# A second copy engine for the first x block, and a 416 + 96 split of the last output piece, in a GEGLU feed-forward kernel

## The chip, the cores and the metric

The kernel runs on one core of one Trainium2 chip. The metric is the device time of one execution in microseconds (us). In the profile, PE is TensorE's matmul work, PEld its weight loads, DVE VectorE, ACT ScalarE and POOL GpSimd; ACTq and SPq are the queues of ScalarE and SyncE that issue DMAs. To evict is to copy a finished sum out of PSUM; the pitch is the time from one matmul's start to the next one's. The profile covers the span from the core's first to its last instruction; it is about 1.8 us shorter than the device time (299.16 and 297.4 us in the profiled run before).

## The reference

```
B, S, D, F = 32, 32, 1024, 3584                     # bf16
def reference(x, w_gate, w_up, w_down):
    return (gelu(x @ w_gate) * (x @ w_up)) @ w_down # gelu with the tanh approximation
```

So 1024 rows of x go through two products of 1024 by 3584 and one of 3584 by 1024.

## The kernel before

The operations are recorded in a list per engine. A helper derives the semaphore waits from the keys that each operation reads (`r`) and writes (`w`). The same key can stand for a PSUM bank: a matmul that writes bank b waits for the engine that last read bank b.

TensorE needs x transposed, with the 1024 input columns in eight blocks of 128 on the partitions. Blocks 2 to 7 come through a transposing DMA. Blocks 0 and 1 are wanted sooner: 512 rows of them are loaded plainly into `xn`, transposed by TensorE into PSUM and copied out. The gate and up matmuls of block 0 come next. The kernel's PSUM tile `ps`, which every matmul writes, has eight banks, and bank 2m (gate) and 2m+1 (up) hold the sums of weight column m = 0..3.

```python
for n in [512] * 6 + [128] * 2:          # warm-up matmuls on constants, bank 3
    pr.add("pe", "matmul", ps[:, 3, 0:n], one[:, 0:P], one[:, 0:n], start=True, stop=True, w=[("ps", 3)])
for i, eng in enumerate(("sp", "act")):  # half of x's first 512 rows on each DMA queue
    pr.add(eng, "dma_start", xn[:, 2*i:2*i+2, :], x_r[:, 2*i:2*i+2, 0:NX*P], w=[("xn", i)], dma=f"xn{i}")
# ... weight and x loads are cut ...
pr.add("act", "activation", warm[:, 0:1], const0, ACTF.Gelu_apprx_tanh)   # brings the table load here
for k in range(NX):                      # NX = 2 blocks
    for i, b in enumerate((6, 7) if k == 0 else (4, 5)):
        half = ps[:, b, 0:P].bitcast(BF16)
        for t in range(2):
            pr.add("pe", "transpose", half[:, t*P:(t+1)*P], xn[:, 2*i+t, k*P:(k+1)*P], ident[:, :],
                   r=[("xn", i), "ident"], w=[("ps", b)])
        pr.add("dve", "tensor_copy", xT[:, k, i*256:(i+1)*256], half, r=[("ps", b)],
               w=[("x", k, 0) if i == 0 else ("x", k, "b")])
# ... the gate, up and most of the down matmuls are cut ...
jobs += [[(TC-1, 0, 512)], [(TC-1, 512, 256)], [(TC-1, 768, 256)]]   # last 128 rows: three pieces
# each piece: 28 matmuls, then a copy from PSUM (ScalarE and VectorE in turn), then its output DMA
```

## Time and profile before

| | before |
|---|---|
| median of 6 runs | 299.86 us (299.33 to 300.19) |
| span of the profiled run | 297.4 us |
| first gate matmul starts | 4.61 us |
| last matmul starts | 294.65 us |
| from there to the end | 2.73 us |

The page of the kernel before gives the busy time of each engine and the shares of the chain of waits that ended last:

```profile
PE 292.7 (98%) x1362; PEld 79.3 (27%) x808; DVE 42.5 (14%) x68; ACT 37.5 (13%) x67; POOL 0.7 (0%) x6
...
PE 98%; issue 0%; ACT 0%
```

In the timeline each line has a start and a duration in us, the engine, the operation and, in brackets, the idle time before it with what ended that idle time. These are the lines of the head of the kernel before, gathered from narrow windows of its timeline (weight loads, matmuls, the first two VectorE copies, ScalarE):

```profile
0.74 0.47 ACTq L98 DMA_DIRECT2D xn<-in_x_dram  x1
...
3.52 1.28 ACT L98 ACT_TABLE_LOAD   x1 [3.52 <-issue]
4.82 0.20 ACT L98 ACTIVATE warm<-const-float32-0.0 128x1 f32<-128x1 f32 x1
...
3.96 0.29 DVE L98 COPY xT<-ps 128x256 bf16<-128x256 bf16 x1 [3.96 <-PE ps L98]
...
4.17 0.29 DVE L98 COPY xT<-ps 128x256 bf16<-128x256 bf16 x1
...
4.58 0.56 PEld L98 LDWEIGHTS ps<-xT,wg 128*128 128x128 bf16 x4 [0.29 <-issue]
...
4.61 0.38 PE L98 MATMUL ps<-xT,wg 128*128 128x512 bf16 x1
```

The second copy ends at 4.47 and the first gate matmul follows at 4.61. Four weight loads follow one another without a wait between them, and a matmul of 512 columns is drawn 0.38 us long. Starts of such matmuls are 215.7 ns apart, which is the measure of their cost; the drawn length overlaps the next one.

The tail of the kernel before, again from its timeline:

```profile
294.65 0.27 PE L98 MATMUL ps<-wd,hT 128*128 128x256 bf16 x1
294.96 0.38 ACT L98 ACTIVATE xT<-ps 128x256 bf16<-128x256 f32 x1 [5.52 <-PE ps L98]
295.37 0.33 SPq L98 DMA_DIRECT2D out_dram<-xT  x1
```

From its groups by shape, the matmuls of the two last pieces (count, then busy us, mean ns, idle us before); then, from its DMA view, the last issue (KB, us to landing):

```profile
L98 PE MATMUL ps<-wd,hT 128*128 128x256 bf16 x56 | 6.3, 272 | 0.0
...
out_dram<-xT SPq DMA_DIRECT2D x1, 64.0 KB, 1.6
```

The last matmul starts at 294.65; ScalarE evicts the piece, the DMA is issued and lands 1.61 us later, and the span ends 0.40 us after that.

### The profile page before, as it was taken

The page shows a single profiled execution, that of the slowest core. Times are in us where ns is not written, and L with a number is a line of the kernel's source. Part 1 is how long each engine was busy: PE and PEld are TensorE (multiplying, and loading weights), DVE is VectorE, ACT ScalarE, POOL GpSimd, SP SyncE. Part 2 cuts the span into 40 slices and gives each one's busy share as a digit, 9 for nine tenths or more (in the row PEclk, how much of TensorE's full clock was granted, in tenths as well). Part 3 has the DMA queues.
Part 4 walks back from the last instruction along what each step waited for, and adds up shares of the span by engine and source line. Part 5 has one row for each costly group of instructions (what it writes and reads, how often), then busy time and mean ns, then how long its engine had stood idle before and what let it go on. Part 6 is the DMA issues. An engine that isn't in the chain of part 4 may idle for free.

```text
span 297.4 us, 2549 instructions
## 1 busy us (share of the span) xinstructions
PE 292.7 (98%) x1362; PEld 79.3 (27%) x808; DVE 42.5 (14%) x68; ACT 37.5 (13%) x67; POOL 0.7 (0%) x6
## 2 busy tenths in 40 slices
PE   8999999999999999999999999999999999999996
PEld 4444222222222222222222222222222222222255
DVE  1030311112211111111111221110000000000000
ACT  1030411111111111211111111110000000000010
POOL 0000000000000000000000000000000000000000
PEclk9999999999999999999999999999999999999999
DMA  7999734006608309121030030000101101001011
GB/s 201 268 247 354 237 106 142 1 0 225 198 2 304 121 10 355 62 102 39 0 141 2 0 141 0 0 2 0 35 0 37 35 0 35 15 23 35 0 35 35
DMA packets 28842, 26.37 MB, mean 89 GB/s; under 512 B 8224, under 2 KB 25248, under 8 KB 28832
## 3 DMA queue, kind: packets, MB, share of 16 engines
q1 hardware_dynamic: 26640, 24.25, 25.5%
q10 hardware_dynamic: 2192, 1.97, 2.3%
q8 instruction: 8, 0.13, 0.2%
q14 instruction: 2, 0.02, 0.0%
HBM read 22.28 MB, written 2.10 MB: 82 GB/s over the span
## 4 chain that ended last, share of the span: by engine, by line
PE 98%; issue 0%; ACT 0%
PE ps L98 56%; PE ps L163 43%; ACT xT L98 0%
## 5 line engine op out<-in xcount | busy, mean ns | idle before, releaser
L98 PE MATMUL ps<-xT,wg 128*128 128x512 bf16 x250 | 88.4, 379 | 0.3
L98 PE MATMUL ps<-xT,wu 128*128 128x512 bf16 x250 | 87.9, 379 | 0.2
L98 PE MATMUL ps<-wd,hT 128*128 128x512 bf16 (+1 forms) x272 | 83.6, 357 | 0.0
L163 PE MATMUL ps<-wd,hT 128*128 128x512 bf16 x196 | 74.3, 379 | 0.4
L163 PE MATMUL ps<-xT,wu 128*128 128x512 bf16 x189 | 71.6, 379 | 0.3
L163 PE MATMUL ps<-xT,wg 128*128 128x512 bf16 x189 | 71.6, 379 | 0.2
L98 DVE TENSOR_TENSOR hT<-g,ps 128x512 bf16<-128x512 f32 x56 | 36.3, 685 | 158.1 <-PE ps L98 152.5
L98 ACT ACTIVATE g<-ps 128x512 f32<-128x512 f32 x56 | 30.8, 595 | 159.8 <-PE ps L98 159.8
L98 PEld LDWEIGHTS ps<-wd,hT 128*128 128x128 bf16 x280 | 27.4, 98 | 69.8 <-issue 65.8
L98 PEld LDWEIGHTS ps<-xT,wu 128*128 128x128 bf16 x256 | 25.0, 98 | 71.7 <-issue 64.1
L98 PEld LDWEIGHTS ps<-xT,wg 128*128 128x128 bf16 x256 | 25.0, 98 | 71.5 <-issue 64.0
L98 DVE CAST xT<-ps 128x512 bf16<-128x512 f32 (+1 forms) x8 | 5.3, 658 | 87.7 <-ACT xT L98 79.8
L98 ACT ACTIVATE xT<-ps 128x512 bf16<-128x512 f32 (+1 forms) x9 | 5.2, 573 | 94.6 <-PE ps L98 94.6
L98 PE MATMUL ps<-const-bfloat16-1.0 128*128 128x512 bf16 (+1 forms) x8 | 2.9, 545 | 0.8 <-PEq L309 0.8
L98 ACT ACT_TABLE_LOAD x1 | 1.3, 1283 | 3.5 <-issue 3.5
L98 PEld LDWEIGHTS ps<-const-bfloat16-1.0 128*128 128x128 bf16 x8 | 1.0, 137 | 2.4 <-issue 2.4
L98 DVE COPY xT<-ps 128x256 bf16<-128x256 bf16 x4 | 0.9, 292 | 4.0 <-PE ps L98 4.0
L98 PE MATMUL ps<-ident,xn 128*128 128x128 bf16 x8 | 1.1, 311 | 0.0
L98 PEld LDWEIGHTS ps<-ident,xn 128*128 128x128 bf16 x8 | 0.8, 136 | 0.0
L98 POOL TENSOR_SCALAR_AFFINE_SELECT ident<-ident 128x128 bf16<-128x128 bf16 x1 | 0.3, 295 | 0.2 <-POOL ident L98 0.2
L98 POOL MEMSET ident<- 128x128 bf16 x1 | 0.2, 205 | 0.3 <-POOLq L309 0.3
L98 ACT ACTIVATE warm<-const-float32-0.0 128x1 f32<-128x1 f32 x1 | 0.2, 203 | 0.0
(4 smaller groups left out, 0.4 us busy)
## 6 DMA issues: line engine op xcount, KB each, us to landing
wd<-in_w_down_dram SPq DMA_DIRECT2D x7, 1024.0 KB, 5.1
wg<-in_w_gate_dram SPq DMA_DIRECT2D x6, 1024.0 KB, 7.8
wu<-in_w_up_dram SPq DMA_DIRECT2D x6, 1024.0 KB, 10.1
out_dram<-xT SPq DMA_DIRECT2D x15, 128.0 KB, 1.7
wg<-in_w_gate_dram ACTq DMA_DIRECT2D x3, 256.0 KB, 4.9
wu<-in_w_up_dram ACTq DMA_DIRECT2D x3, 256.0 KB, 5.2
wu<-in_w_up_dram ACTq DMA_DIRECT2D x2, 128.0 KB, 3.8
wg<-in_w_gate_dram SPq DMA_DIRECT2D x2, 128.0 KB, 3.3
```

The lines of the kernel that those rows point to most:

```text
L98: ins = name(eng, *args, **kw) if callable(name) else getattr(eng, name)(*args, **kw)
L163: return eng.add_instruction(mybir.InstMatmult(start_tensor_calc=start, stop_tensor_calc=stop, ldweights=False, name=nc.get_next_instructi ...
```

## The change

There are two intents. In the head, the second half of block 0 is copied out by two engines at once, so that the first gate matmul can start sooner; for this ScalarE's table load is moved to the very front. In the tail, the last piece shrinks to 96 columns, so that less is left to evict and to store when TensorE is done.

```diff
+        pr.add("act", "activation", warm[:, 0:1], const0, ACTF.Gelu_apprx_tanh)   # now ahead of the DMA issues
 ...
-        pr.add("act", "activation", warm[:, 0:1], const0, ACTF.Gelu_apprx_tanh)
         for k in range(NX):
-            for i, b in enumerate((6, 7) if k == 0 else (4, 5)):
-                (two transposes of 128 columns into bank b, one VectorE copy of 256)
+            plan = ([((0, 1), 6, "dve"), ((2,), 7, "dve"), ((3,), 5, "act")] if k == 0 else
+                    [((0, 1), 4, "dve"), ((2, 3), 2, "dve")])
+            (per entry: its transposes into its bank, then one copy by the engine named)
 ...
-        jobs += [[(TC - 1, 0, 512)], [(TC - 1, 512, 256)], [(TC - 1, 768, 256)]]
+        jobs += [[(TC - 1, 0, 512)], [(TC - 1, 512, 416)], [(TC - 1, 928, 96)]]
```

The two lines in parentheses shorten code. One further key, `("x", k, "c")`, makes the first half of the matmuls wait for ScalarE's copy as well.

## The prediction

> What bounds it now. TensorE: the page gives PE 98% busy, and the chain of waits is 98% PE. In the timeline the first gate matmul starts at 4.61 us and the last matmul at 294.65; 1344 matmuls of 512 columns (or their equal) at the traced 215.7 ns are 289.9 us of that. The middle has no slack; only the head (4.6 us) and the tail (about 2.6 us) can change.
>
> Head, before. The timeline has the transposes at a 107 ns pitch from 3.51; the four 256-column copies on VectorE start at 3.96, 4.17, 4.39, 4.60 (292 ns each), each as soon as its second transpose is done. PE's last transpose starts at 4.25; PE then waits for the second copy (ends 4.47) and goes on at 4.61. The first gate weights had landed at 4.01. At most about 0.25 us can be won.
>
> Head, after. ScalarE's copy of 128 columns, estimated from traced ACTIVATEs (597 ns at 512, 384 at 256), takes about 0.28 us; its transpose is seen done at 4.17, so it ends at 4.45, against 4.47. That gains 0.02 us, and an extra wait in PE's queue (76 ns) may eat it. Two costs are added:
> - The second copy of block 1 moves from bank 5 to bank 2, which the second gate matmul writes. The copy ends near 4.89; the matmul wants to start at about 4.81. I expect a stall of 0.1 to 0.15 us.
> - The table load (1283 ns) and warm-up activation now stand before ScalarE's DMA issues. The second half of x landed at 3.62 with no slack. If the queue runs ahead of the engine, the issues move by some 0.05 us. The Trainium skill (Perfetto Trace Analysis, Per-instruction lifecycle, DVE / Act Engine Instruction) says the sequencer fetches on once an instruction is in the wait queue; the trace agrees so far as the warm-up activation starts 11 ns after the table load ends, but no DMA issue follows a running activation there. If it blocked (20%), x and the up weights would come 1.4 us later.
>
> Tail. The last pieces go from 256 + 256 to 416 + 96 columns. The traced pitch (109 ns at 256, 215.7 at 512) is columns/2.4 plus 2.4 ns; 416 + 96 cost the same sum if 96 columns reach 42 ns with a weight load each. The Trainium skill (TensorE: Matmul & The Clock Gate, Back-to-back issue gap) gives 81 ns as sustained at 128 columns; this trace shows no warm pitch below 256. At 50 ns the loss is 0.2 us, at 81 it is 1.1. The last eviction shrinks from 384 ns to about 250 (estimate, same slope), gaining 0.13 us; the last DMA's 1.6 us from issue to landing is nearly all fixed.
>
> Sum: head +0.1, tail about 0. Predicted 299.9 us, range 299.2 to 301.2; chances: faster by over 2% 0.002, within 2% 0.993, slower by over 2% 0.005.
>
> What would show it, all in the timeline: ScalarE's first DMA issue (about 0.8, or 2.2 if it blocks); the ends of the x copies; the first gate matmul (4.55 to 4.7) and its gap to the second (215 ns if bank 2 costs nothing, about 300 if it does); the pitch of the 96-column matmuls; the last ACTIVATE (about 250 ns) and the time from its end to the span's end (2.0 us, unchanged).
>
> What would make it wrong: a blocking table load; a 96-column pitch set by the weight load; slow 192-byte writes; a different moment at which TensorE's clock rises in the head; run-to-run spread (0.56 us here).

## The result and the profile after

The median is 299.88 us (299.11 to 300.54, 6 runs) against 299.86. The ratio is 1.000, with a 95% interval of 0.998 to 1.002. The spans are 297.5 and 297.4 us. The predicted time (299.9) was met. But equal times do not say that nothing happened: both ends changed, and the profile shows more than one surprise.

The engine shares after:

```profile
PE 293.1 (99%) x1362; PEld 77.8 (26%) x808; DVE 42.7 (14%) x68; ACT 37.6 (13%) x68; POOL 0.7 (0%) x6
```

The head after, the same windows of the timeline:

```profile
0.74 1.28 ACT L98 ACT_TABLE_LOAD   x1 [0.74 <-PEq L317]
0.80 0.46 ACTq L98 DMA_DIRECT2D xn<-in_x_dram  x1
...
2.03 0.20 ACT L98 ACTIVATE warm<-const-float32-0.0 128x1 f32<-128x1 f32 x1
...
4.19 0.28 ACT L98 ACTIVATE xT<-ps 128x128 bf16<-128x128 bf16 x1 [1.95 <-PE ps L98]
...
3.96 0.29 DVE L98 COPY xT<-ps 128x256 bf16<-128x256 bf16 x1 [3.96 <-PE ps L98]
...
4.17 0.21 DVE L98 COPY xT<-ps 128x128 bf16<-128x128 bf16 x1
...
4.61 0.29 DVE L98 COPY xT<-ps 128x256 bf16<-128x256 bf16 x1
...
4.58 0.10 PEld L98 LDWEIGHTS ps<-xT,wg 128*128 128x128 bf16 x1 [0.27 <-issue]
4.96 0.18 PEld L98 LDWEIGHTS ps<-xT,wg 128*128 128x128 bf16 x2 [0.28 <-DVE xT L98]
...
4.61 0.59 PE L98 MATMUL ps<-xT,wg 128*128 128x512 bf16 x1
...
4.99 0.62 PE L98 MATMUL ps<-xT,wg 128*128 128x512 bf16 x1
```

Four things are to be read here. The DMA is issued at 0.80, 0.06 us later than before, while the table load runs from 0.74 to 2.02: the load does not hold the queue back. The copy on ScalarE ends at 4.46, where the old second copy ended at 4.47. The second gate matmul starts 380 ns after the first, not 215, and the weight load before it is said to wait for VectorE, whose last copy ends at 4.90 and empties bank 2. But the matmuls are also drawn 0.59 and 0.62 us long instead of 0.38: the trace's clock record begins, at full clock, at 5.47 us in this run, against 4.59 in the run before. (It has no row for the time before; the profile's view by stretches prints 1.00 there. That TensorE runs at half clock until then is read from its pitch: 427 ns for 512 columns among the warm-up matmuls, 215.7 later.) So two explanations for the 380 ns stand side by side.

The tail after, from its timeline:

```profile
295.12 0.21 PE L98 MATMUL ps<-wd,hT 128*128 128x96 bf16 x1
295.36 0.25 ACT L98 ACTIVATE xT<-ps 128x96 bf16<-128x96 f32 x1 [5.52 <-PE ps L98]
295.64 0.33 SPq L98 DMA_DIRECT2D out_dram<-xT  x1
```

From its groups by shape, the matmuls of the last piece; from its DMA view, the last issue:

```profile
L98 PE MATMUL ps<-wd,hT 128*128 128x96 bf16 x28 | 1.4, 206 | 0.0
...
out_dram<-xT SPq DMA_DIRECT2D x1, 24.0 KB, 1.4
```

The last matmul starts at 295.12 and 2.35 us remain, against 2.73. Of the 0.38 us, 0.07 are only the shorter last matmul, whose columns moved to the piece before: at columns/2.4 plus 2.4 ns, all matmuls together cost the same, but the last one starts 0.067 us later. The real gain is 0.31 us: 0.133 from the eviction (384 to 251 ns), 0.177 from the DMA, which took 1.63 us from issue to the end of the wait for it, and now 1.45.

The sum explains the spans in ns: first gate matmul 5 earlier; 476 more from it to the last matmul (410 in the head, 66 from the later start of the last one); 377 less from there to the end. That is +94, and the spans differ by 297,473 - 297,379 = 94. The head seems to give back all that the tail gains. The question for the experiments is whether that 0.41 us is the change's doing.

### The profile page after: what moved, and what is told of

Its sections match the earlier page's. It is cut to its first block, busy times and chain, and to the rows that moved or that the text cites. A ratio compares the mean times of both kernels' runs of the same rounds, so it can differ in the third digit from the quotient of the medians.

```text
span 297.5 us, 2550 instructions
## 1 busy us (share of the span) xinstructions
PE 293.1 (99%) x1362; PEld 77.8 (26%) x808; DVE 42.7 (14%) x68; ACT 37.6 (13%) x68; POOL 0.7 (0%) x6
## 4 chain that ended last, share of the span: by engine, by line
PE 95%; SPq 2%; DMA 2%; issue 1%; ACT 0%
PE ps L98 52%; PE ps L163 43%; SPq L98 2%; DMA xT<-in_x_dram 2%; ACT xT L98 0%
## 5 line engine op out<-in xcount | busy, mean ns | idle before, releaser
L98 PE MATMUL ps<-wd,hT 128*128 128x512 bf16 (+2 forms) x272 | 83.6, 357 | 0.0
L98 PEld LDWEIGHTS ps<-wd,hT 128*128 128x128 bf16 x280 | 25.9, 98 | 71.4 <-issue 65.8
L98 ACT ACTIVATE xT<-ps 128x512 bf16<-128x512 f32 (+2 forms) x10 | 5.3, 530 | 96.5 <-PE ps L98 96.5
L98 DVE COPY xT<-ps 128x256 bf16<-128x256 bf16 (+1 forms) x4 | 0.9, 272 | 4.0 <-PE ps L98 4.0
L98 ACT ACT_TABLE_LOAD x1 | 1.3, 1283 | 0.7 <-PEq L317 0.7
```

What stands on the lines that cost most here:

```text
L98: ins = name(eng, *args, **kw) if callable(name) else getattr(eng, name)(*args, **kw)
```

## The experiments

Each kernel ran beside runs of the kernel before on the same chip; e1 to e4, e5 to e8, e9 to e12 ran on three chips. "Rise" is the moment at which the trace's clock record begins to show full clock. "Lost early" is the sum of what matmul starts in the first 3 us after the first gate matmul fall behind their full-clock pitch, whatever the cause (in e3 and e10 it is the wait for bank 2, in the others the low clock); "lost to DMA" is the same later in the head, where the waits name a load. The third column is the time from the fourth transpose (the last of block 0) to the first gate matmul; in e9, and near their end in e11, the clock rose during the transposes, which shortens it there. All are computed from the start times in the traces, in ns unless marked us.

| kernel | rise, us | 4th transpose to gate | 1st to 2nd gate | lost early | lost to DMA | last matmul to end | span, us |
|---|---|---|---|---|---|---|---|
| before | 4.59 | 786 | 215 | 0 | 0 | 2730 | 297.38 |
| after | 5.47 | 769 | 380 | 406 | 0 | 2353 | 297.47 |
| e1_bank1 | 5.64 | 769 | 379 | 498 | 193 | 2339 | 297.72 |
| e2_tail_only | 4.70 | 786 | 215 | 0 | 0 | 2351 | 297.23 |
| e3_head_only | 4.44 | 769 | 338 | 133 | 0 | 2704 | 297.57 |
| e4_after_again | 5.45 | 769 | 380 | 408 | 0 | 2338 | 297.44 |
| e5_before_again | 4.83 | 786 | 304 | 88 | 433 | 2705 | 297.87 |
| e6_tail64 | 5.36 | 790 | 382 | 351 | 0 | 2369 | 297.45 |
| e7_split_first | 5.25 | 567 | (split) | 367 | 0 | 2343 | 297.30 |
| e8_bank1_again | 4.82 | 774 | 309 | 93 | 0 | 2352 | 297.15 |
| e9_tail_again | 3.93 | 771 | 215 | 0 | 0 | 2344 | 297.04 |
| e10_after_third | no record | 769 | 341 | 136 | 1072 | 2353 | 298.26 |
| e11_split_again | 4.50 | 531 | (split) | 0 | 0 | 2342 | 297.08 |
| e12_no_warmup | no record | 788 | 378 | 1358 | 0 | 2718 | 298.98 |

### e1_bank1: the bank alone

```diff
-                    [((0, 1), 4, "dve"), ((2, 3), 2, "dve")])
+                    [((0, 1), 4, "dve"), ((2, 3), 1, "dve")])
```

> The changed kernel with one number changed: the second copy of block 1 leaves bank 1 instead of bank 2, and bank 1 is first written by the fifth matmul, not the second. Theory (the bank is a new wait): the gap from the first to the second gate matmul falls from 380 ns to the plain pitch (215 ns, or about 427 ns if TensorE's clock is still low at that moment), no wait on VectorE in front of the second matmul, and about 0.15 us less span than the changed kernel at the same clock moment. Rival (the 380 ns are the low clock alone): the gap stays at 380 or more.

The gap stayed: 379 ns, with the second weight load issued at 4.59, right behind the first matmul, and no wait. From its timeline:

```profile
4.55 0.14 PEld L98 LDWEIGHTS ps<-xT,wg 128*128 128x128 bf16 x2 [0.27 <-issue]
...
4.59 0.59 PE L98 MATMUL ps<-xT,wg 128*128 128x512 bf16 x1
```

Bank 2 was therefore not what set the 380 ns of the first profile of the change; my first reading of it falls, and the rival holds for that run. At half clock a matmul of 512 columns that starts after idle time takes some 380 ns until the next (the first warm-up matmul shows 381), and the following ones 427. Times: 299.75 us median, ratio 1.000 (0.9986 to 1.0014), which tells nothing.

### e3_head_only, e4_after_again, e8_bank1_again, e10_after_third: does bank 2 cost anything

e3 is the changed kernel with the old tail, e4 and e10 are the changed kernel once more, e8 is e1 once more.

```diff
 e3:
-        jobs += [[(TC - 1, 0, 512)], [(TC - 1, 512, 416)], [(TC - 1, 928, 96)]]
+        jobs += [[(TC - 1, 0, 512)], [(TC - 1, 512, 256)], [(TC - 1, 768, 256)]]
```

> The changed head with the old tail (256 + 256). Theory (bank 2 stall): some 0.15 us slower than before from the stall alone, 0.4 us if the late clock rise also belongs to the head's change; the first gate matmul still starts at 4.6 us. Rival (the head is neutral): within 0.1 us of before and a gap of 215 ns after the first gate matmul.

> The changed kernel once more, unchanged. If the moment at which TensorE's clock rises in the head (about 5.5 us in the first profile of it, about 4.5 in the one of before) is chance from run to run, it will differ here; if the change causes it, it is again near 5.5. The stall of about 165 ns before the second gate matmul comes back either way (in time until its weight load starts: near 4.95 us).

> Bank 1 instead of bank 2 once more, unchanged, for its head in a run in which the clock may rise early. If it rises before 4.7 us: a gap of about 215 ns after the first gate matmul, where the changed head with bank 2 had 338. If it rises late: 380 ns again, which is the low clock, and nothing is learnt of the bank.

> The changed kernel, third time. Theory (tail -0.30, copies -0.02, bank stall 0.12 where the clock has risen early and nothing where it has not, clock moment by chance): the mean of all its runs is 0.2 to 0.3 us below before, with a spread of about 1.5 us. Rival (no gain at all): pooled mean equal to that of before.

e3 caught a run in which the clock had risen early. Its weight loads and first two matmuls, from its timeline:

```profile
4.66 0.10 PEld L98 LDWEIGHTS ps<-xT,wg 128*128 128x128 bf16 x1 [0.27 <-issue]
5.03 0.11 PEld L98 LDWEIGHTS ps<-xT,wg 128*128 128x128 bf16 x2 [0.27 <-DVE xT L98]
...
4.69 0.38 PE L98 MATMUL ps<-xT,wg 128*128 128x512 bf16 x1
...
5.03 0.39 PE L98 MATMUL ps<-xT,wg 128*128 128x512 bf16 x1
```

The matmuls have their full-clock length (0.38), and the second still waits until VectorE's copy out of bank 2 has ended at 4.97. That wait costs 133 ns. e10 shows it again: 136 ns, matmuls of 0.38 us, the second weight load at 4.92 after a copy that ended at 4.87. Every old head with an early rise (before, e2, e9) has 215 ns there. In e8, with bank 1, the clock rose between the first and second matmul; here are its weight loads:

```profile
4.56 0.14 PEld L98 LDWEIGHTS ps<-xT,wg 128*128 128x128 bf16 x2 [0.27 <-issue]
4.90 0.10 PEld L98 LDWEIGHTS ps<-xT,wg 128*128 128x128 bf16 x1 [0.20 <-DVE xT L98]
```

Now the first two loads go one behind the other, so the second matmul waits for nothing; its 309 ns are the low clock of the first. (e5, an old head in which the clock rose 219 ns after the first gate matmul's start, as against 230 here, has 304. The third load is put down to VectorE because a wait on it sits there, but it starts 1 ns after the second matmul, as the loads of the kernel before do.) So bank 2 costs 0.13 us when the clock is up, and nothing when it is not (380 ns with bank 2, 379 with bank 1), because the first matmul then lasts as long as the copy. No run with bank 1 had the clock up before the first gate matmul. e8 ran once, at 298.93 us; its state is unknown, and it is one draw from a wide spread.

My expectation for e4, that a stall of 165 ns "comes back either way", was wrong as to its cause: the 380 came back, and it was the clock. e4 had a ratio of 0.998 (0.9968 to 0.9993; median 299.29), e10 one of 1.0015 (0.9999 to 1.003; 299.84), and both are the same kernel, so the interval is too narrow to judge 0.2% by. Against the before-runs, the mean of the changed kernel was 0.00, -0.62 and +0.39 us: my expectation of a pooled gain of 0.2 to 0.3 is not shown by the times (the mean of the three is -0.08). e3 had 299.47 and a ratio of 0.9999 (0.9979 to 1.002), its mean being pulled up by one run of 301.35.

### e2_tail_only and e9_tail_again: the tail alone

The kernel before, with the new line of `jobs` and nothing else.

```diff
-        jobs += [[(TC - 1, 0, 512)], [(TC - 1, 512, 256)], [(TC - 1, 768, 256)]]
+        jobs += [[(TC - 1, 0, 512)], [(TC - 1, 512, 416)], [(TC - 1, 928, 96)]]
```

> The kernel before with only the new tail (416 + 96 columns). Theory (the tail gains, the head gives it back): the part of the span from the last matmul's start to the end is 2.35 us against 2.73 before, the 96-column pitch is 42.5 ns, and the time is some 0.3 us (0.1%) below before: 299.5. Rival (the tail is neutral, as predicted): within 0.1 us of before.

> Old head with the 96-column tail, once more, beside the changed kernel and the split on one chip. Theory: 2.35 us from the last matmul's start to the end, 0.3 us below before on the sum of both places; the time 299.4 to 299.6. Rival (the gain of the first time was chance): the ratio to before is 1.000 or above.

In both traces the remainder after the last matmul's start is 2.35 and 2.34 us, and in e3, with the old tail, it is 2.70. The nine traces with 96 columns (2338 to 2353) and the four of the old tail (2704 to 2730) do not overlap. The 96-column matmuls start 42.5 ns apart. So the tail gains 0.30 us in every trace (377 less 66 in the first pair; 0.30 between the means of the groups). The times agree in one call and not in the other: 299.41 with a ratio of 0.9987 (0.9973 to 1.0001), then 299.62 and 1.0002 (0.9989 to 1.0015), which is what the rival of e9 named. The gain is shown in the traces and not in the times.

### e6_tail64: how small may the last piece be

```diff
-        jobs += [[(TC - 1, 0, 512)], [(TC - 1, 512, 416)], [(TC - 1, 928, 96)]]   # on top of e2
+        jobs += [[(TC - 1, 0, 512)], [(TC - 1, 512, 448)], [(TC - 1, 960, 64)]]
```

> The kernel before with the tail 448 + 64. Pitch theory (columns/2.4 plus 2.4 ns): 29.1 ns at 64 columns, and the sum of the last two pieces is unchanged. Rival (a floor set by the weight load): clearly more, 40 ns or above. Last ACTIVATE about 225 ns. From the last matmul's start to the end: 2.30 us if the last output DMA is free to go, or longer than the 2.35 of the 96-column tail if the 448-column piece, evicted by VectorE in about 625 ns and issued on the same queue, now holds it up.

The pitch is 29.1 ns: still columns/2.4 plus 2.4, with a weight load before each matmul and no floor. The remainder is 2369 ns, more than with 96 columns although the eviction is shorter. The two last DMA issues, from its timeline:

```profile
295.15 0.81 SPq L98 DMA_DIRECT2D out_dram<-xT  x2
```

The last eviction, from its groups by shape:

```profile
L98 ACT ACTIVATE xT<-ps 128x64 bf16<-128x64 f32 x1 | 0.2, 225 | 5.5 <-PE ps L98 5.5
```

The two issues lie one close behind the other, from 295.15 to 295.95; the second starts on time, 25 ns after the eviction, but takes 393 ns instead of 332. The packets of the 448-column piece run until 296.45, and the first packet of the last piece starts at 296.47, 0.91 us after its issue (0.83 with 96 columns). Most of that 0.08 us, 0.06, is the longer issue itself. I read this as the large piece being in the way of the small one, at the issue more than in the packets; it was not tested by moving either to another queue. Of the two sizes, 64 gains nothing over 96 in the trace. The time was 299.36, ratio 0.9977 (0.9964 to 0.999), a mean 0.65 us below before, more than this tail can give by its trace.

This run also bears on the clock. Its head is the old one, and yet the rise came at 5.36 us, with a gap of 382 ns and 351 ns lost. Its first two gate matmuls, from its timeline:

```profile
4.61 0.59 PE L98 MATMUL ps<-xT,wg 128*128 128x512 bf16 x1
...
4.99 0.56 PE L98 MATMUL ps<-xT,wg 128*128 128x512 bf16 x1
```

A late rise does not need the changed head, so the 0.41 us of the first pair cannot be put down to the change on this evidence. Whether it comes as often with both heads is open: it came after 5.2 us in three of the five changed heads that have a record, and in two of the seven others.

### e5_before_again: chance in the kernel before

> The kernel before, unchanged. Theory (the moment at which TensorE's clock rises is chance[...]): the rise can come at any moment from some 4.4 to 5.7 us, so it may be late here too, and then the first gate matmuls run at a pitch near 427 ns and the span grows by half the delay (up to 0.5 us) with nothing else changed. Rival (the changed head causes the late rise): the rise is before 4.7 us as in the first profile of this kernel.

The rise was at 4.83, between the two groups: inconclusive on that point. But the trace shows a second source of chance. From its waits between 7.5 and 13.5 us (engine, what it waited for, sum in us, times, longest):

```profile
PEld ps L98 <- DMA wg<-in_w_gate_dram: 0.8, 2, 0.5
PEld ps L98 <- DMA wu<-in_w_up_dram: 0.5, 1, 0.5
```

TensorE lost 433 ns because loads for blocks 2 and 3 landed late; the waits name the gate and up weights, and x of block 2 landed at nearly the same moment. e10 lost 1072 ns in the same way, which is why its span is 298.26. The time of e5 was 299.89, ratio 0.9992 (0.998 to 1.0004).

### e12_no_warmup: what the clock's rise hangs on

```diff
-        for n in [512] * 6 + [128] * 2:
-            pr.add("pe", "matmul", ps[:, 3, 0:n], ...)
```

> The kernel before without the eight warm-up matmuls on constants. Theory (the clock rises 3.65 to 4.9 us after TensorE starts its work, and until then each matmul takes twice as long, so the loss is half of the delay): TensorE starts at about 3.5 us, the rise comes between 7.1 and 8.4 us, and the time lost to the low clock after the first gate matmul is 1.25 to 1.9 us, so the span is 1.2 to 1.9 us longer, except where late x blocks would have made it wait anyway. Rival (the rise does not depend on TensorE's work): the rise is again between 4.4 and 5.7 us and the span is unchanged.

From the groups by shape of the window from 4.8 to 7.3 us, first this kernel, then the kernel before (last columns: busy us, mean ns):

```profile
L98 PE MATMUL ps<-xT,wg 128*128 128x512 bf16 x4 | 1.9, 622 | 0.0
L98 PE MATMUL ps<-xT,wu 128*128 128x512 bf16 x2 | 1.1, 634 | 0.0
```

```profile
L98 PE MATMUL ps<-xT,wg 128*128 128x512 bf16 x8 | 2.0, 378 | 0.0
L98 PE MATMUL ps<-xT,wu 128*128 128x512 bf16 x5 | 1.4, 379 | 0.0
```

Six matmuls fit where thirteen did before. The trace has no clock record, but the pitch turns to 216 ns near 7.6 us, 3.8 us after TensorE's first work at 3.76, and the loss is 1358 ns, half of the delay from 4.86. It was expected at 1.25 to 1.9. The time was 300.76 (one run). In the other late runs the same rule holds: after, (5.47 - 4.61)/2 = 0.43 against 0.41; e6, 0.37 against 0.35. The clock follows TensorE's work, as far as this one run without warm-up shows; with warm-up its rise came 3.2 to 4.9 us after that work began at 0.78.

### e7_split_first and e11_split_again: taking away the wait itself

The change shortens the copy. This experiment lets TensorE work during it: the old head and the 96-column tail, but the first two gate matmuls are cut into halves of 256 columns. The first halves need only the first copy. Parentheses shorten code.

```diff
+        def mm_half(m, i):
+            c0 = i * 256
+            pr.add("pe", "matmul", ps[:, 2*m, c0:c0+256], (gate weights of m, block 0), xT[:, 0, c0:c0+256],
+                   start=(i == 0), stop=False, r=[(weights), ("x", 0, "b" if i else 0)], w=[("ps", 2*m)])
 ...
+    for i in range(2):           # instead of the two matmuls m = 0, 1 of block 0
+        for j in range(2):
+            mm_half(j, i)
```

With `start` in the first half only, the result is correct.

> Old head and 96-column tail, but the first two gate matmuls are split into halves of 256 columns, first halves first, so that TensorE need not wait for the second copy of block 0. Theory (the wait for the second copy is on the critical path): the first gate matmul starts near 4.40 us instead of 4.61 to 4.78, and 0.2 us of idle time goes; the span is 0.2 us below the tail-only kernel at the same clock moment, 0.1 if the clock is still low then. Rival (it only moves the wait): a gap of the same size appears before the second halves or at the third matmul.

> The split of the first two gate matmuls with the 96-column tail, once more. Theory: from the start of the fourth transpose to the first gate matmul 0.57 us against 0.79 in every old head and 0.77 in every changed one, so the lowest span where the clock rises early (about 297.0), and a ratio to before of 0.998. Rival: the wait comes back behind the first halves.

The time from the fourth transpose to the first gate matmul falls from 786 to 567 and 531 ns, and no wait appears behind the halves: e11, with an early rise, loses nothing. From its timeline:

```profile
4.02 0.72 PE L98 MATMUL ps<-ident,xn 128*128 128x128 bf16 x6
4.63 0.60 PE L98 MATMUL ps<-xT,wg 128*128 128x256 bf16 x4
```

The four halves run as one block, 109 ns apart. (Here x itself landed late, so that the start is at 4.63 in spite of the gain. For the same reason the span of e11 is not the lowest, as I had expected: 297.08 against 297.04 in e9, whose fourth transpose started 0.28 us earlier.) The clock's moment alone changes e7 by 0.37. Times: 299.50, ratio 0.9985 (0.9971 to 1.0000), and 299.25, ratio 0.9995 (0.9978 to 1.0011). By the traces it beats both kernels: with the clock early and loads in time, the sum of head, tail and matmuls is lower than before by 0.24 (head) + 0.30 (tail) = 0.54 us, less 0.01 for the extra matmuls. The times point the same way but do not prove it: each interval reaches 1.000, and the ratio of 0.998 that I expected of e11 did not come.

## Why the prediction was right, and where not

- **What bounds it.** Right: TensorE is 99% busy after, and every difference found lies before 16 us or after the last matmul.
- **ScalarE's copy, a gain of 0.02 us.** Right: 786 to 769 ns from the fourth transpose to the first gate matmul, in all changed heads but one (774). Half of the columns hardly helps: the copy of 256 columns took VectorE 292 ns, the one of 128 takes ScalarE 277. The extra wait of 76 ns did not come: one wait instruction in TensorE's queue holds both semaphores.
- **Bank 2, a stall of 0.10 to 0.15 us.** The mechanism and the size are right where the clock is up (133 and 136 ns, absent with bank 1 and in old heads). What the prediction did not see is that a late rise hides it. The test it named, a gap of "about 300 if it does", gave 380 for another reason; a gap alone does not tell the two apart, the drawn length of the matmul does.
- **Table load, 20% risk of 1.4 us.** The likely side came: the issue moved by 0.06 us (estimate 0.05), and DMAs go out while the load runs, as the Trainium skill (Perfetto Trace Analysis, Per-instruction lifecycle) let one expect.
- **Pitch at 96 columns.** The formula read from 256 and 512 columns held (42.5 ns, and 29.1 at 64); the feared 81 ns did not come.
- **Last eviction, -0.13 us.** Right: 384 to 251 ns.
- **"The last DMA's 1.6 us from issue to landing is nearly all fixed."** This step was wrong, a mis-sized term: it fell from 1.63 to 1.45 us, and "the time from its end to the span's end (2.0 us, unchanged)" from 2.04 to 1.86. The 128 data packets took 27.2 ns each at 512 bytes and 14.9 at 192, eight to an engine, which makes 0.10 us; another 0.07 lies between the last packet and the landing (0.43 and 0.36 us); why that part shrank was not tested.
- **The sum.** "Head +0.1, tail about 0" should read head +0.12 or -0.02 (early or late clock), tail -0.30, so some 0.2 to 0.3 us of gain. The predicted 299.9 agrees with the measured 299.88, but the measurement can't tell +0.1 from -0.3: its interval is 0.6 us on either side. The forecast that the time would stay within 2% rests on solid ground; the agreement to 0.1 us is chance.
- **What the prediction listed as able to upset it**, a different moment of the clock's rise and the run-to-run spread, is larger than what was to be measured. In 14 traces the loss to a low clock was 0 to 0.50 us with warm-up, and the loss to late loads 0 to 1.07. Late loads occurred in two of the six changed heads in which the table load comes first, and in one of eight others; whether the 0.06 us later issue has a part in that is open. For the gate weights of blocks 2 and 3 on ScalarE's queue, little of the lag is left: they were issued at 2.28 to 2.29 us in changed heads and at 2.27 to 2.28 in the others, and landed anywhere from 7.36 to 8.90.

## What to carry to other kernels

When a kernel is bound by one engine from end to end, a change can pay only in the head and the tail; add up both from start times in the trace, because a gain of 0.1% drowns in a spread of 0.5%. Before a buffer is moved to another bank, ask who writes that bank next. Rather than shorten a copy that an engine waits for, give the engine work that needs only the part already there: the split won 0.24 us where the faster copy won 0.02.

## What the Trainium skill lacked or had wrong

- "TensorE: Matmul & The Clock Gate", Back-to-back issue gap: it gives 81 ns as the sustained spacing of 128-column matmuls with a weight load each, and 131 ns at 512 columns. Here 512 columns ran at 215.7 ns, 96 columns ran at 42.5 ns and 64 at 29.1 with a weight load each, as the page's own formula for the isolated gap has it. At 128 columns itself there is a short stretch in e9: where the clock rose among the transposes, the last three started 55 and 56 ns apart with a weight load each.
- The same page, The HAM clock gate: it says that the window of 3413 ns runs free of the kernel and that the transition comes around 4 us of activity. The runs agree on the middle (the rise came 3.2 to 4.9 us after the first matmul) and on the window (the full clock then lasted 293.546 us, 86 such windows, in the traces that have the record). But the page's spread, 500 ns to either side, is too narrow: here it was 1.7 us from the earliest to the latest. A late rise cost up to 0.50 us here, and 1.36 without warm-up.
- "Perfetto Trace Analysis", DVE / Act Engine Instruction: it lets one expect, but does not say, that a DMA issue may pass a running ScalarE instruction. It may: issue at 0.80 us, table load from 0.74 to 2.02.
- "ScalarE: Activation LUTs", What ACT_TABLE_LOAD costs: the 1283 ns agree, but the drain of about 1380 ns that it adds is not in these traces, whose only load is the first one; the next activation starts 11 ns after it. A later switch of tables was not measured.
- "DMA: Bandwidth & Descriptors", Specifications: it gives 512 bytes as the least size for full rate, with read-modify-write below. As a rate the runs agree: the 192-byte output packets took 14.9 ns against 27.2 for 512 bytes, which is 12.9 against 18.8 bytes per ns. What it lacks is that the smaller packet still ended sooner, which is what counts for a last small store (1.45 against 1.63 us to the end of the wait).
